# An eight-expert layer between attention and a token mixer: experts with few slots take their hidden parts two at a time

## The chip, the cores and the metric

The kernel runs on one core of a Trainium2 chip. Its time is device time in microseconds (us): the median of three runs before the change is 499.38 us (497.16 to 500.8). One profiled execution, 495.95 us long, gives all the rows below; its span from the first to the last instruction is 494.1 us.

## The reference, cut to what matters

Three layers follow each other: local attention, a mixture of experts, and a mixer over tokens and channels. The change is in the second, whose core is this:

```
for b in range(B):                     # B, S, D, E, F = 2, 768, 512, 8, 1024
    for s in range(S):
        e = fresh_e or prev_e          # arg max of the gate, or the expert of the token before
        p = softmax(logits[b, s])
        h = np.maximum(x[b, s] @ w1[e], 0.0)
        out[b, s] = p[e] * (h @ w2[e])
```

Each of the 1536 tokens goes to one of eight experts. An expert has a 512 by 1024 matrix `w1`, a relu, and a 1024 by 512 matrix `w2`.

## The kernel before, in words

**Slots.** The experts are ranked by how many tokens they have. Expert of rank `r` gets `RCAP[r]` slots: 288, 256, 256, 256, 192, 192, 160, 160. A tile of rows is 128 slots; rank 0 has three tiles, the others two. In ranks 4 to 7 the second tile has only 64 or 32 slots, and in rank 0 the third has 32. Ranks 4 to 7, with `N <= FEW = 192` slots, are the "few-slot" experts.

**Parts.** The 1024 hidden columns of an expert are eight parts of 128, so that the loop at L1564 runs over 64 units `u = 8 * r + f`. Weights come in pieces of two parts, 512 KB of `w1` and 512 KB of `w2` each, three buffers deep (`NRAW`). `load_piece` issues their DMAs on SP's queue: the `w1` half of a piece when the first products that read its last predecessor are issued, the `w2` half at the end of `mm2` of an odd unit.

**A unit, in program order.** Every engine executes its own instructions in this order; an order of different engines is set by semaphores alone.

- `mm1(u + 2)` (L1429): first products, slots as columns. In ranks 0 to 3 each is twelve TensorE products of split weights (L1454). In ranks 4 to 7 the raw float32 weights are used, four products that the trace shows as eight matmuls (L1438). Each unit takes a PSUM bank of its own from pool `pB`, which has two.
- `mm2(u)` (L1478): second products. A whole tile of rows takes three matmuls 512 columns wide (L1491) over the 128x128 array. A tile of 64 or 32 slots takes another form (L1501): the array is used as two or four column tiles side by side, each with 64 or 32 columns of weights, and each makes a part of the output columns (256 or 128). These are float32, and the trace shows two matmuls for each.
- `split_w1(u + 3)` and `split_w2(u + 1)`: ACT rounds the raw weights to a high half (L1324, L1421), DVE subtracts for the low half (L1325, L1422). Few-slot experts need no `split_w1`.
- `relu(u + 2)` (L1457): ACT makes the high half `hh` of the whole tiles (L1468), DVE the part tile `hx` (L1472) and the low half `hl` (L1473).
- `y_out(u)`: ACT scales a finished tile of the expert before, and issues its store.
- `tick()`, six times in a unit: 2.4 steps a unit (ranks 4 to 7) of a side job that decodes matrices of the third layer. A job is six steps, mostly DVE instructions on 128x512 (L396 to L408), an ACT copy at each end (L395, L405), and a DMA of the next 512 KB, issued on ACT's queue (L381).
- `x_tr(r + 1, i)` (L1287), at parts 2 and 3: four TensorE transposes of a tile of the next expert's rows (L1299), an ACT copy (L1302), and the gather of the tile three further on by GpSimd.

Ahead of the loop stand `mm1(0)`, `relu(0)`, `mm1(1)`, `split_w1(2)`, `split_w2(0)`, `relu(1)`, in this order (L1556 to L1561). `LOADS` (L74) orders the first weight DMAs after that of piece 0's `w1`: `(1, 1)` is the `w1` half of piece 1, `(0, 2)` the `w2` half of piece 0.

Of the kernel before, what the change touches and what calls it, by code (L numbers as in the profile page):

```python
# [38 lines left out]
FEW = 192  # L39
RBASE = [1, 4, 6, 8, 10, 12, 14, 16]  # L40
# [33 lines left out]
LOADS = ((1, 1), (0, 2), (1, 2), (2, 1), (2, 2))  # L74
# [14 lines left out]
def f32(ap):  # L89
    return ap.bitcast(F32)  # L90
# [3 lines left out]
def kernel(  # L94
# [887 lines left out]
    def load_piece(n, parts=(1, 2)):  # L982
# [4 lines left out]
        k = r if n else -1  # L987
        if k not in regs:
            regs[k] = SP.value_load(order_g[0:1, r : r + 1] if n else first_i, min_val=0, max_val=E - 1)
# [287 lines left out]
    wsp1, mb_, pR_ = {}, [], []  # L1277
# [9 lines left out]
    def x_tr(r, i, low=True):  # L1287
# [8 lines left out]
        tp = (pR_[0] if r else pZ).tile([128, 4, 128], F32, tag="tr", name="tr")  # L1296
# [45 lines left out]
    with ExitStack() as mctx:  # L1342
# [5 lines left out]
        pR_.append(pR)  # L1348
        pslot = {}
# [75 lines left out]
        hts = {}  # L1425

        hps = {}

        def mm1(u):  # L1429
# [4 lines left out]
            hp = pB.tile([128, 512], F32, tag="b", name="h")  # L1434
            if N <= FEW:
                x, o = f32(xTs[r][0]), u % 2
# [10 lines left out]
            else:  # L1447
                h1, l1 = wsp1.pop(u)
# [6 lines left out]
            hps[u] = hp  # L1455

        def relu(u):  # L1457
# [4 lines left out]
            hp = hps.pop(u)  # L1462
            hh = mb.tile([128, max(RCAP)], F32R, tag="hh", name="hh", bufs=4)
            hl = mb.tile([128, max(RCAP)], F32R, tag="hl", name="hl", bufs=4)
            n, hx = N // 128 * 128, None
            if width(r, RTILES[r] - 1) == 128:
                n = N
            A.activation(hh[:, :n], hp[:, :n], AF.Relu)  # L1468
            if n < N:

                hx = mb.tile([128, 64], F32, tag="hx", name="hx", bufs=4)
                V.tensor_scalar(hx[:, : N - n], hp[:, n:N], 0.0, None, op0=ALU.max)  # L1472
            V.scalar_tensor_tensor(hl[:, :n], hp[:, :n], 0.0, f32(hh[:, :n]), op0=ALU.max, op1=ALU.subtract)  # L1473
            hts[u] = (hh, hl, hx)

        yps = {}

        def mm2(u):  # L1478
# [4 lines left out]
            hh, hl, hx = hts.pop(u)  # L1483
            for i in range(RTILES[r]):
# [3 lines left out]
                c = width(r, i)  # L1488
                if c == 128:
# [8 lines left out]
                else:  # L1498
                    W = 4 * c
                    for g in range(128 // c):  # L1500
                        PE.matmul(  # L1501
                            out[g * c : g * c + M, :W],
                            lhsT=hx[:, :M],
                            rhs=w[:, g * W : (g + 1) * W],
                            start=(f == 0),
                            stop=(f == 7),
                        )
            if u % 2:
                pieces.pop(u // 2)
                load_piece(u // 2 + NRAW, (2,))  # L1510
# [480 lines left out]
```

## Time and profile before

| what | value |
|---|---|
| median of three runs | 499.38 us |
| profiled execution | 495.95 us, span 494.1 us |
| TensorE (PE) busy | 478.5 us, 97% of the span |
| VectorE (DVE) busy | 353.8 us, 72% |
| ScalarE (ACT) busy | 260.8 us, 53% |
| granted TensorE clock | 0.999 of full speed |
| DMA | 83.18 MB, 168 GB/s mean |

Busy shares are averages over three layers with different limits. The expert loop runs from about 121 to 309 us. Where rows give starts of consecutive TensorE instructions, the distance between starts is what an instruction takes of the engine; the duration printed beside it also holds the time in which the array empties and overlaps the next one.

### The profile page before, as it was taken

The page shows a single profiled execution, that of the slowest core. Times are in us where ns is not written, and L with a number is a line of the kernel's source. Part 1 is how long each engine was busy: PE and PEld are TensorE (multiplying, and loading weights), DVE is VectorE, ACT ScalarE, POOL GpSimd, SP SyncE. Part 2 cuts the span into 40 slices and gives each one's busy share as a digit, 9 for nine tenths or more (in the row PEclk, how much of TensorE's full clock was granted, in tenths as well). Part 3 has the DMA queues.
Part 4 walks back from the last instruction along what each step waited for, and adds up shares of the span by engine and source line. Part 5 has one row for each costly group of instructions (what it writes and reads, how often), then busy time and mean ns, then how long its engine had stood idle before and what let it go on. Part 6 is the DMA issues. An engine that isn't in the chain of part 4 may idle for free.

```text
span 494.1 us, 9501 instructions
## 1 busy us (share of the span) xinstructions
PE 478.5 (97%) x3328; PEld 385.0 (78%) x3330; DVE 353.8 (72%) x955; ACT 260.8 (53%) x634; POOL 117.4 (24%) x145
## 2 busy tenths in 40 slices
PE   8998998899999999999999999999999999999994
PEld 4676776678788899987777776888888888888884
DVE  6878878857665878777777888657999795751421
ACT  5977786732455756665455664555655354520300
POOL 4003214234105303021311102303453232430400
PEclk9999999999999999999999999999999999999999
DMA  8967578713949876976888995420012000000122
GB/s 244 350 191 247 178 242 248 227 44 114 337 63 299 287 255 227 303 253 225 297 278 288 305 312 174 142 98 22 23 64 72 15 23 21 2 34 32 34 96 69
DMA packets 62343, 83.18 MB, mean 168 GB/s; under 512 B 6496, under 2 KB 40928, under 8 KB 62288
## 3 DMA queue, kind: packets, MB, share of 16 engines
q1 hardware_dynamic: 53812, 61.97, 39.4%
q10 hardware_dynamic: 5708, 13.50, 8.0%
q0 software_dynamic: 2768, 7.02, 4.6%
q8 instruction: 28, 0.46, 0.4%
q14 instruction: 27, 0.22, 0.1%
HBM read 71.14 MB, written 11.34 MB: 167 GB/s over the span
## 4 chain that ended last, share of the span: by engine, by line
PE 79%; DVE 7%; DMA 6%; ACT 4%; issue 2%; ACTq 0%; SPq 0%; DVEq 0%; POOLq 0%
PE a L1746 21%; PE o L1491 11%; PE h L1454 8%; PE b L1783 7%; PE th L1670 6%; PE h L1438 6%; PE s L547 3%; PE x L626 3%; PE o L1501 3%; PE pt L602 2%; DVE sm L569 2%; DMA yd<-yo 2%; DMA jraw<-in_w_tokT_dram 2%; PE h L757 2%; PE y L768 2%
## 5 line engine op out<-in xcount | busy, mean ns | idle before, releaser
L1746 PE MATMUL a<-wtokr,z 128*128 128x512 f32 x480 | 87.1, 340 | 0.0
L1746 PEld LDWEIGHTS a<-wtokr,z 128*128 128x128 f32 x480 | 73.5, 188 | 10.7
L1491 PE MATMUL o<-w2s,hh 128*128 128x512 f32 x192 | 64.9, 417 | 0.7 <-DVE w2s L1422 0.4
L579 ACT ACTIVATE pr<-sm,st 128x256 f32<-128x256 f32 (+1 forms) x96 | 46.1, 482 | 19.9 <-DVE st L569 19.9
L1422 DVE TENSOR_TENSOR w2s<-raw,w2s 128x512 fp32r<-128x512 f32 x64 | 44.0, 688 | 14.7 <-ACT w2s L1421 14.6
L1454 PE MATMUL h<-xT,w1s 128*128 128x256 f32 (+1 forms) x384 | 53.4, 288 | 1.2 <-DVE w1s L1325 0.6
L1454 PEld LDWEIGHTS h<-xT,w1s 128*128 128x128 f32 x384 | 49.5, 188 | 4.3 <-DVE w1s L1325 1.1
L1438 PE MATMUL h<-xT,raw 128*128 128x192 f32 (+1 forms) x256 | 46.0, 323 | 0.0
L1438 PEld LDWEIGHTS h<-xT,raw 128*128 128x128 f32 x256 | 38.5, 190 | 7.0 <-issue 6.6
L1421 ACT ACTIVATE w2s<-raw 128x512 fp32r<-128x512 f32 x64 | 39.9, 623 | 7.6 <-ACT yo L1537 3.5
L569 DVE CUSTOM_DVE_ANT_0 sm<-s,bias 128x256 f32<-128x256 f32 (+1 forms) x96 | 34.0, 395 | 10.3 <-PE s L547 10.1
L1468 ACT ACTIVATE hh<-h 128x256 fp32r<-128x256 f32 (+1 forms) x64 | 20.8, 324 | 33.8 <-PE h L1454 18.9
L1491 PE MATMUL o<-w2s,hl 128*128 128x512 f32 x96 | 38.0, 395 | 0.0
L1491 PEld LDWEIGHTS o<-w2s,hh 128*128 128x128 f32 x192 | 33.0, 189 | 5.2 <-DVE w2s L1422 1.2
L1012 POOL DMA_INDIRECT xg<-xd,xidx x17 | 16.8, 986 | 85.0 <-PE tr L1299 78.6
L602 PE MATMUL pt<-ident,pr 128*128 128x128 f32 x176 | 26.0, 280 | 4.5 <-DVE xt L652 3.2
L1325 DVE TENSOR_TENSOR w1s<-raw,w1s 128x512 fp32r<-128x512 f32 x32 | 22.1, 690 | 9.6 <-ACT w1s L1324 9.4
L1791 DVE SCALAR_TENSOR_TENSOR ob<-b,xTf 128x512 f32<-128x512 f32 (+1 forms) x16 | 8.8, 556 | 27.6 <-PE b L1783 27.5
L1702 POOL TENSOR_TENSOR si<-si,yg 128x512 f32<-128x512 f32 x10 | 13.4, 1343 | 60.0 <-ACT si L1695 50.8
L1473 DVE SCALAR_TENSOR_TENSOR hl<-h,hh 128x256 fp32r<-128x256 f32 (+1 forms) x64 | 22.4, 350 | 6.0 <-ACT hh L1468 6.0
L602 PEld LDWEIGHTS pt<-ident,pr 128*128 128x128 f32 x176 | 19.2, 141 | 9.4 <-DVE xt L652 3.8
L547 PE MATMUL s<-kall,q 64*128 64x256 f32 (+1 forms) x192 | 25.6, 385 | 0.0
(266 smaller groups left out, 951.3 us busy)
## 6 DMA issues: line engine op xcount, KB each, us to landing
raw<-in_w_dram SPq DMA_DIRECT2D x64, 512.0 KB, 5.2
vv<-in_pack_dram SPq DMA_DIRECT2D x10, 512.0 KB, 5.7
jraw<-in_w_tokT_dram ACTq DMA_DIRECT2D x10, 512.0 KB, 4.7
w<-in_w_dram SPq DMA_DIRECT2D x16, 256.0 KB, 6.6
kall<-in_pack_dram SPq DMA_DIRECT2D x10, 320.0 KB, 4.4
xd<-xt SPq DMA_DIRECT2D x12, 256.0 KB, 2.1
q<-in_pack_dram SPq DMA_DIRECT2D x11, 256.0 KB, 4.5
yd<-yo ACTq DMA_DIRECT2D x11, 256.0 KB, 4.1
```

What stands on the lines that cost most here:

```text
L547: PE.matmul(sp[hh][:, 0:W], lhsT=qs[n][half, j], rhs=kall[half, b, j, t * 160 + 160 - W : t * 160 + 160], start=True, stop=True,)
L569: V.tensor_tensor_reduce(out=sm[:, hh, 0:W], in0=ust[u]["s"][hh], in1=bias[:, 2 * j + hh], scale=-0.125, scalar=BIG, op0=ALU.add, op1=ALU.min,
L579: A.activation(pr[:, hh, 0:W], sm[:, hh, 0:W], AF.Exp, bias=st[:, hh : hh + 1], scale=-1.0, accum_out=sums[n][:, 2 * j + hh : 2 * j + hh + 1],
L602: PE.transpose(pt[:, hh, c], pr[:, hh, c * 128 : (c + 1) * 128], ident)
L1421: A.activation(h2, bb[:, o], AF.Copy)
L1422: V.tensor_tensor(l2, bb[:, o], f32(h2), op=ALU.subtract)
L1438: PE.matmul(hp[:, :N], lhsT=pieces[u // 2][1][:, j, o * 128 : (o + 1) * 128], rhs=x[:, j, :N], start=(j == 0), stop=(j == 3),)
L1454: PE.matmul(hp[:, :N], lhsT=wa[:, j], rhs=xa[:, j, :N], start=(k == 0), stop=(k == 11))
L1491: PE.matmul(out[:M], lhsT=ha[:, lo : lo + M], rhs=wa, start=(f == 0 and q == 0), stop=(f == 7 and q == 2),)
L1670: PE.matmul(th, lhsT=xa[:, j], rhs=wa[:, j], start=(n == 0), stop=(n == 11))
L1746: PE.matmul(acc[b][d][o], lhsT=za[:, d * 128 : (d + 1) * 128], rhs=wa[:, lo:hi], start=(t == 0 and n == 0 and (o == 0 or d % 2 == 0)), sto ...
L1783: PE.matmul(op[:, : hi - lo], lhsT=wa[:, d, e * 128 : (e + 1) * 128], rhs=ua[d][:, lo:hi], start=(n == 0), stop=(n == 11),)
```

## The change

Part tiles are multiplied for two parts in a row, everywhere: `mm2` does the whole tiles alone, and a new `mm2_few` does the part tile of units `u` and `u + 1`. In ranks 0 to 3 it is called at the end of `mm2` of an odd unit. In ranks 4 to 7 the loop body runs for a pair of units at once: both `mm1`, both `mm2`, then `mm2_few`. A pair's first products share a bank (two halves of 256 columns), and one ACT and two DVE instructions do the relu of both. `split_w2` runs two units ahead. Both tiles of the next expert's rows are transposed at part 2, the second one into a bank of pool `pO`. The twelve ticks of a pair remain twelve.

Beside this, `LOADS` puts the `w2` half of piece 0 ahead of the `w1` half of piece 1, and at `u = 0` the call `mm1(2)` stands behind `mm2(0)`. The lines ahead of the loop are the same.

```diff
+FEW0 = 4
-LOADS = ((1, 1), (0, 2), (1, 2), (2, 1), (2, 2))
+LOADS = ((0, 2), (1, 1), (1, 2), (2, 1), (2, 2))
...
-        k = r if n else -1
+        k = r if n or parts != (1,) else -1
...
-        tp = (pR_[0] if r else pZ).tile([128, 4, 128], F32, tag="tr", name="tr")
+        if r > FEW0 and i:
+            tp = pO_[0].tile([128, 4, 128], F32, tag="o", name="tr")
+        else:
+            tp = (pR_[0] if r else pZ).tile([128, 4, 128], F32, tag="tr", name="tr")
...
         def mm1(u):
-            hp = pB.tile([128, 512], F32, tag="b", name="h")
+            o = u % 2
             if N <= FEW:
-                x, o = f32(xTs[r][0]), u % 2
+                if o == 0:
+                    hps[u] = pB.tile([128, 2, 256], F32, tag="b", name="h")
+                hp = hps[u - o][:, o]
+                x = f32(xTs[r][0])
...
         def relu(u):
+            few = N <= FEW
+            if few and u % 2 == 0:
+                return
+            hp = hps.pop(u - 1 if few else u)
...
+            if few:
+                dh, dl = [x[:, : 2 * n].rearrange("p (i c) -> p i c", i=2) for x in (hh, hl)]
+                A.activation(dh, hp[:, :, :n], AF.Relu)
+                V.tensor_scalar(hx[:, :, : N - n], hp[:, :, n:N], 0.0, None, op0=ALU.max)
+                V.scalar_tensor_tensor(dl, hp[:, :, :n], 0.0, f32(dh), op0=ALU.max, op1=ALU.subtract)
+                for o in range(2):
+                    hts[u - 1 + o] = hh[:, o * n : o * n + n], hl[:, o * n : o * n + n], hx[:, o]
+                return
...
+        def mm2_few(u):
+            r = u // 8
+            i = RTILES[r] - 1
+            c, M, out = width(r, i), RCAP[r] - i * 128, yps[r][i]
+            for v in (u, u + 1):
+                hx, w = fews.pop(v)
+                for g in range(128 // c if c < 128 else 0):
+                    PE.matmul(
+                        out[g * c : g * c + M, : 4 * c],
+                        lhsT=hx[:, :M],
+                        rhs=w[:, 4 * g * c : 4 * (g + 1) * c],
+                        start=(v % 8 == 0),
+                        stop=(v % 8 == 7),
+                    )
+            pieces.pop(u // 2)
+            load_piece(u // 2 + NRAW, (2,))
...
+            if RCAP[r] > FEW:
+                if u:
+                    mm1(u + 2)
+                mm2(u)
+                if u % 2:
+                    mm2_few(u - 1)
+                if u == 0:
+                    mm1(2)
...
+            elif u % 2 == 0:
+                mm1(u + 2)
+                mm1(u + 3)
+                if f == 2 and r < 7:
+                    for i in range(2):
+                        x_tr(r + 1, i)
+                mm2(u)
+                mm2(u + 1)
+                mm2_few(u)
+                split_w2(u + 2)
+                for _ in range(3):
+                    tick()
+                relu(u + 3)
+                for _ in range(3):
+                    tick()
+                split_w2(u + 3)
+                y_out(u)
+                for _ in range(6):
+                    tick()
+                y_out(u + 1)
```

## Rows read from the trace of the kernel before

**Rows 1.** Page, busy time of each engine: us, share of span, instructions.

```profile
PE 478.5 (97%) x3328; PEld 385.0 (78%) x3330; DVE 353.8 (72%) x955; ACT 260.8 (53%) x634; POOL 117.4 (24%) x145
```

**Rows 2.** Stretches of the expert loop: length, busy per engine, clock, DMA share, GB/s.

```profile
121.00:170.00 49.00, 47.25 (x340) 38.80 (x338) 31.03 (x71) 26.09 (x55) 12.80 (x12) 1.00 0.80 240
...
222.00:267.00 45.00, 45.00 (x253) 33.46 (x251) 33.86 (x82) 23.35 (x51) 8.72 (x8) 1.00 0.82 272
267.00:304.00 37.00, 37.00 (x293) 27.25 (x290) 31.35 (x82) 23.29 (x51) 4.51 (x5) 1.00 0.88 293
```

**Rows 3.** Waits of TensorE, 121 to 310 us: line, releaser, total, times, longest.

```profile
PE h L1454 <- DVE w1s L1325: 0.6, 2, 0.4
...
PE o L1491 <- DVE w2s L1422: 0.4, 2, 0.2
```

**Rows 4.** Timeline of TensorE, around rank 4's first units: start, duration, what.

```profile
221.53 1.46 PE L1438 MATMUL h<-xT,raw 128*128 128x192 f32 x8
222.69 0.75 PE L1491 MATMUL o<-w2s,hh 128*128 128x512 f32 x2
223.28 0.39 PE L1491 MATMUL o<-w2s,hl 128*128 128x512 f32 x1
223.51 0.62 PE L1491 MATMUL o<-w2s,hh 128*128 128x512 f32 x2
...
228.65 0.40 PE L1491 MATMUL o<-w2s,hl 128*128 128x512 f32 x1
228.98 0.65 PE L1501 MATMUL o<-raw,hx 128*64 128x256 f32 x4
229.56 1.57 PE L1438 MATMUL h<-xT,raw 128*128 128x192 f32 x8
230.83 0.76 PE L1491 MATMUL o<-w2s,hh 128*128 128x512 f32 x2
```

**Rows 5.** The same timeline in rank 6.

```profile
274.30 0.43 PE L1501 MATMUL o<-raw,hx 128*32 128x128 f32 x8
274.65 1.35 PE L1438 MATMUL h<-xT,raw 128*128 128x160 f32 x8
...
276.64 0.42 PE L1501 MATMUL o<-raw,hx 128*32 128x128 f32 x8
```

**Rows 6.** Chain of waits at 118 us: float32 products 128 (L757), 256 (L768) wide.

```profile
118.39 0.89 PE h L757 x8
119.28 1.73 PE y L768 x8
```

**Rows 7.** The same chain at the loop's start: start, us, what.

```profile
122.01 5.90 DMA raw<-in_w_dram
...
128.65 0.70 DVE w2s L1422
...
129.40 1.43 PE o L1491 x5
```

**Rows 8.** Timelines of ACT and TensorE there; brackets: idle before, releaser.

```profile
125.00 0.62 ACT L1324 ACTIVATE w1s<-raw 128x512 fp32r<-128x512 f32 x1
127.99 0.63 ACT L1421 ACTIVATE w2s<-raw 128x512 fp32r<-128x512 f32 x1 [2.36 <-DMA raw<-in_w_dram]
...
125.03 3.33 PE L1454 MATMUL h<-xT,w1s 128*128 128x288 f32 x23 [0.21 <-DVE w1s L1325]
128.67 0.50 PE L1491 MATMUL o<-w2s,hh 128*128 128x512 f32 x1 [0.31 <-ACT w2s L1421]
...
131.12 1.86 PE L1454 MATMUL h<-xT,w1s 128*128 128x288 f32 x12
```

**Rows 9.** Chain of waits and TensorE's timeline, late in the loop.

```profile
280.55 7.76 DMA jraw<-in_w_tokT_dram
...
288.34 0.68 ACT jm L395
...
306.68 0.50 PE L1491 MATMUL o<-w2s,hh 128*128 128x512 f32 x1 [0.18 <-DVE w2s L1422]
```

More of the change, by code (lines that the diff above doesn't have):

```diff
@@ L1348 @@
         pR_.append(pR)
+        pO_.append(pO)
         pslot = {}
@@ L1447, in mm1 @@
             else:
+                hps[u] = hp = pB.tile([128, 512], F32, tag="b", name="h")
                 h1, l1 = wsp1.pop(u)
@@ L1461, in relu @@
             N = RCAP[r]
[L1462 removed]
+            n = N // 128 * 128
+            if width(r, RTILES[r] - 1) == 128:
+                n = N
+            few = N <= FEW
+            if few and u % 2 == 0:
+                return
+            hp = hps.pop(u - 1 if few else u)
             hh = mb.tile([128, max(RCAP)], F32R, tag="hh", name="hh", bufs=4)
             hl = mb.tile([128, max(RCAP)], F32R, tag="hl", name="hl", bufs=4)
[L1465 to L1467 removed]
+            if n < N:
+                if few or u % 2 == 0:
+                    hxs[0] = mb.tile([128, 2, 64], F32, tag="hx", name="hx", bufs=2)
+                hx = hxs[0]
+            if few:
[6 more added lines that the diff above has]
+                return
             A.activation(hh[:, :n], hp[:, :n], AF.Relu)
             if n < N:
[L1471 to L1472 removed]
+                V.tensor_scalar(hx[:, u % 2, : N - n], hp[:, n:N], 0.0, None, op0=ALU.max)
             V.scalar_tensor_tensor(hl[:, :n], hp[:, :n], 0.0, f32(hh[:, :n]), op0=ALU.max, op1=ALU.subtract)
[L1474 to L1476 removed]
+            hts[u] = hh, hl, hx[:, u % 2] if n < N else None
+        yps, fews = {}, {}
         def mm2(u):
@@ L1497, in mm2 @@
                         )
[L1498 to L1510, printed above, removed]
+        def mm2_few(u):
[14 more added lines that the diff above has]
+            load_piece(u // 2 + NRAW, (2,))
         def y_out(u):
@@ L1571, in tick @@
                     quick[0] %= 1
-            mm1(u + 2)
-            mm2(u)
-            tick()
-            split_w1(u + 3)
-            tick()
-            split_w2(u + 1)
-            tick()
-            tick()
-            relu(u + 2)
-            tick()
-            tick()
-            y_out(u)
+            if RCAP[r] > FEW:
[7 more added lines that the diff above has]
+                tick()
+                split_w1(u + 3)
+                tick()
+                split_w2(u + 1)
+                if u == 8 * FEW0 - 1:
+                    split_w2(u + 2)
+                tick()
+                tick()
+                relu(u + 2)
+                tick()
+                tick()
+                y_out(u)
[8 more added lines that the diff above has]
+                mm2_few(u)
+                split_w2(u + 2)
+                for _ in range(3):
+                    tick()
+                relu(u + 3)
+                for _ in range(3):
+                    tick()
+                split_w2(u + 3)
+                y_out(u)
+                for _ in range(6):
+                    tick()
+                y_out(u + 1)
             if GX <= u < GX + RTILES[0]:
@@ L1609 @@
             i = f - (2 if r else XF)
-            if r < 7 and 0 <= i < RTILES[r + 1]:
+            if r < FEW0 and 0 <= i < RTILES[r + 1]:
                 x_tr(r + 1, i)
```

12 lines of the change are left out of this document (5 added, 7 removed).

## The prediction

> **What bounds the kernel now.** I read the engines' busy times first: TensorE is at 97%, DVE at 72%, ACT at 53% [rows 1]. A share over three layers says little, so the expert loop was cut into stretches next. From 222 to 304 us, where the few-slot experts run, TensorE is busy all the time at full clock; DVE is busy for 31.35 of the last 37.00 us and the DMA engines are at 0.82 and then 0.88 [rows 2]. TensorE's waits in the whole loop are some 0.4 to 0.6 us each and most stand at its start [rows 3]. So in this loop a change is worth what it takes off TensorE, as long as the next two (DVE, then DMA, in the last two ranks) keep up. The change leaves the number of matmuls as it is. What remains is their order, so I then read TensorE's timeline for what an order costs: the distances between starts.
>
> **What a change of form costs.** The products over the whole array follow each other at 0.23 us (223.28 to 223.51). From the last of them to the first of the part tile there are 0.33 us (228.65 to 228.98): **0.10 us going in**. Eight first products take 1.16 us behind a whole-array product (221.53 to 222.69) and 1.27 us behind a part tile (229.56 to 230.83): **0.11 us coming out** [rows 4]. Inside, the part tile of rank 4 takes 0.58 us (228.98 to 229.56) [rows 4], that of rank 6 0.35 us (274.30 to 274.65) [rows 5]. Elsewhere float32 products of 256 columns run at 1.73 / 8 = 0.216 us and those of 128 at 0.89 / 8 = 0.111 us [rows 6]. With two column tiles at once rank 4's four matmuls would stream in 2 x 0.216 = 0.43 us, with four at once rank 6's eight in 2 x 0.111 = 0.22 us; the rest, 0.15 and 0.13 us, is filling and emptying at the ends, if it isn't inherent in the form.
>
> Two part tiles in a row drop one going in and one coming out, 0.21 us for certain by these rows, and of the rest between nothing and 0.15 us. A merge is thus worth 0.21 to 0.36 us. I take 0.30, nearer to the upper end, because the rows with full streaming are of the same engine and type.
>
> **The sum, part by part.**
>
> - *Merges in ranks 4 to 7*: 32 units, 16 merges, all on the path: 16 x 0.30 = **-4.8 us** (bounds -3.4 and, with 0.36 and 0.34 for the two forms, -5.6).
> - *Merges in rank 0*, which has a part tile of 32 slots: 4 x 0.30 = **-1.2 us** (-0.8, -1.4). The other three ranks have none.
> - *Paired relu*: 32 instructions each of three kinds become 16 of double width. ACT and DVE save part of this, but TensorE waits for neither there [rows 3]: nothing by itself. The even part's relu now waits for the odd part's first products, some 1.2 us [rows 4]; its cover is what lies up to its use, the second products and the part tiles of the pair and the first products of the next, about 4.3 us of the 2 x 2.34 us that a pair takes (274.30 to 276.64) [rows 5]. Queued behind the waiting relu on ACT and DVE are six ticks, a `w2` split and the stores; TensorE needs that split some 4 us later.
> - *Transposes*: the same eight a time, moved ahead of the pair's second products. They no longer stand behind a part tile; both orders change form as often within 0.1 us, three times: nothing. ACT's queue stops for them until the pair's first products are done, where the relu would have stopped it. The second bank comes from `pO`, whose last user there was scaled out two pairs earlier. GpSimd's gathers follow them, three tiles ahead of need: nothing.
> - *Weight DMAs*: each half is issued once in a pair as before, the `w2` half after the merged part tiles. SP is moved past nothing else. The `w2` split needs it two pairs later. Nothing, while DMA keeps up.
> - *DVE and DMA in the last two ranks*: a pair that goes from 4.68 to 4.38 us meets 31.35 / 37.00 x 4.68 = 4.0 us of DVE work, and a DMA share of 0.88 that becomes 0.94 [rows 2, 5]. One side-job load there took 7.76 us to land, and ACT took it up at once when it had (288.34) [rows 9]: what shortens a pair here is partly waited for again. I give back 40% of these eight merges: **+1.0 us** (0 to +2.4). The 0.18 us that TensorE waits for a split `w2` at 306.68 [rows 9] should go, since the splits run earlier: **-0.2 us**.
> - *The loop's start.* Before, the `w1` half of piece 1 is split on ACT at 125.00; then ACT idles 2.36 us until the `w2` half of piece 0 has landed, 5.90 us after its issue [rows 7, 8]. TensorE meanwhile does `mm1(1)` and `mm1(2)`, 23 of whose matmuls follow 125.03 without a break in 3.33 us (12 of them some 1.6 us, without the last one's emptying), and waits 0.31 and 0.23 us beside that. With the DMAs exchanged (SP still loads the same two registers, the second of them before the first of these DMAs, as now), `w2` lands first, but `split_w1(2)` still stands ahead of `split_w2(0)` in ACT's order, and its half now lands second. If that is at 127.99 again, ACT does 0.62 + 0.63 us, DVE two subtractions of 0.70 us [rows 7, 8], so that the second of the products now at 129.40 comes at about 130.05: 0.65 us later; and the 1.6 us of `mm1(2)`, which filled the wait, come behind it: +2.25 us in all. If the second half lands by about 126 us, where the first products of part 1 end, only some 0.15 us are lost. Between these, since a load of 512 KB at the 240 GB/s of this stretch [rows 2] needs 2.2 us behind one that landed by 125.0: landing at 127.2, **+1.4 us** (0.15 to 2.25).
>
> In all -4.8 - 1.2 + 1.0 - 0.2 + 1.4 = **-3.8 us**, from 495.95 us of the profiled execution to 492.1 us. That execution is 3.4 us under the median shown, 499.38 us; on the median's scale the forecast is **495.6 us**.
>
> **A rule against it.** The Trainium skill, "PSUM — Partial Sum Buffer", section "PSUM bank collisions raise a hardware error", says that two engines must not touch one bank in the same 32 partitions at once, even at other columns, so sharing a bank forces the relu of the first half to wait for the second. No run here shows a bank touched by two; the rows show only that the wait of 1.2 us has about 4.3 us of cover. By the rule alone, with that wait on the path in each of 16 pairs, the sum would come out 16 x 1.2 = 19 us the other way; by the rows it comes to nothing.
>
> **The rivals.**
>
> *The start is not late and every merge counts.* The half lands early (+0.15) and all 20 merges give their full value, 8 x 0.36 + 12 x 0.34 = 7.0 us: -7.0 + 0.15 - 0.2 = -7.0 us, 492.4 us. For it: two loads issued within a microsecond may land nearly together. Against: 125.0 and 127.9 before [rows 7, 8].
>
> *The extra belongs to the narrow form, and the start is late.* Merging then gives 0.21 a time, the last two ranks give back half of theirs, and the start costs 2.25: -4.2 + 0.8 + 2.25 = -1.1 us, 498.2 us: the change would not do what it says, as far as can be measured. For it: no row shows two part tiles in a row. Against: the 0.11 us depend on what stood before, for the same matmuls [rows 4].
>
> *The relu comes too late (slower).* In the last two ranks, a pair's relu is released at once for both parts, behind a `w2` split and ticks on ACT and DVE; DVE's work of 4.0 us a pair and the cover of 4.3 us lie close. When ACT waits for a side-job load as late as 7.76 us [rows 9], the relu passes its cover. It decides from a delay of 4.3 us on. If TensorE waits 0.5 us in each of 16 pairs: -6.0 + 8.0 + 1.4 = +3.4 us, 502.8 us. For it: ACT met that load just in time. Against: before, the cover was of the same size, and TensorE waited 0.18 us in it.
>
> **How the numbers follow.** Forecast 0.50, first rival 0.22, second 0.20, third 0.08. One per cent, 5 us, is about what a measurement of this kernel can tell from no change. Under 494.4 us lie a quarter of the forecast's case (its own range is 493.2 to 497.8) and most of the first rival's: 0.33. Over 504.4 us lies part of the third: 0.06. The rest is 0.61. The range that holds 8 in 10 goes from 491.8 us, 0.6 us under the first rival, to 499.6 us, which takes in the second rival.
>
> **What would show it.** In the trace after: distances between starts of 8 part-tile matmuls of rank 4 in a row (1.0 us forecast, 1.16 if nothing but the ends is saved); first products behind them at 1.27 once a pair and 1.16 the other time; a pair in some 5.2 us in rank 4 and 4.4 in rank 6; `mm2(0)`'s second product at about 130 us or later, and `mm1(2)` behind it; waits of TensorE for `hl` or `w2s` in ranks 6 and 7 if the third rival holds; the landing time of side-job loads there. Wrong would be the forecast if the part tiles in a row kept 0.58 and 0.35 us each with all their ends, if TensorE waited over 1 us in the last ranks, or if the start lost nothing.

## The result, and the profile after

The changed kernel takes **501.45 us** (median of 12 runs, 496.89 to 504.25) beside 499.01 us (496.66 to 501.0) of the kernel before on the same chip: **1.0064 times as long, with a 95% interval of 1.0041 to 1.0086**. That is within the 1% that the prediction called no change, but the interval leaves out 1, the sign is the other one, and the time lies above the range (491.8 to 499.6 us). The profiled execution of after has 501.50 us and a span of 499.7 us, 5.6 us more than before (494.1 us).

The two profiled executions are not alike: that of after lies at its median, that of before (495.95 us) under the lowest of its twelve runs. By the medians the change costs 2.4 us, by the ratio 3.2 us; the rows below explain the 5.6 us between these two executions. The granted clock of TensorE is part of what differs from run to run. Its median is 0.9885 in the twelve runs of after, and 0.994 to 0.997, by chip, in the runs of the kernel before that stand beside the experiments. A clock lower by 0.0075 (0.996 less 0.9885) for 500 us can cost 3.75 us at most (an estimate), as much as the whole difference.

On the page, the busy times and the row of the granted clock by slices of 12.5 us (in tenths; 9 stands for 0.9 and more):

```profile
PE 479.0 (96%) x3328; PEld 390.6 (78%) x3330; DVE 349.2 (70%) x923; ACT 259.0 (52%) x618; POOL 115.9 (23%) x145
...
PEclk9999999999799999999999999999999999999999
```

Against [rows 1], ACT and DVE have lost the 16 and 32 instructions of the paired relus, and TensorE is as busy as before. New is the 7 in the clock's row: the slice that begins at 125 us. Three stretches of the loop, to be laid beside [rows 2] (length, busy time and count of PE, PEld, DVE, ACT, POOL, clock, DMA share, GB/s):

```profile
121.00:137.00 16.00, 12.40 (x64) 10.43 (x63) 6.75 (x16) 5.59 (x13) 2.88 (x3) 0.79 0.83 283
222.00:267.00 45.00, 45.00 (x264) 37.18 (x263) 31.44 (x65) 22.85 (x45) 8.71 (x9) 1.00 0.85 281
267.00:304.00 37.00, 36.53 (x293) 28.91 (x293) 31.39 (x69) 21.39 (x43) 2.68 (x3) 1.00 0.90 298
```

From 222 to 267 us more matmuls fit into the same time (264 for 253): the merges work. At the start the clock is down to 0.79, and late in the loop TensorE idles. Its waits from 115 to 320 us say for whom (line, releaser, total, times, longest), beside [rows 3]:

```profile
PE o L1513 <- ACT w2s L1427: 3.0, 1, 3.0
PE tr L1403 <- DVE hit L1398: 0.9, 1, 0.9
PE o L1513 <- DVE w2s L1428: 0.7, 2, 0.5
PE o L1513 <- DVE hl L1488: 0.6, 1, 0.6
...
```

One wait of 3.0 us is new at the start; the three rows below it all stand in rank 7. Where the 5.6 us arise is read from the starts of a few TensorE instructions, `mm1(u)` standing for the first product of unit `u`. Here and below such starts are rounded to 0.1 us before they are subtracted, so that a difference is good to 0.1 us:

| span, us | before | after | difference |
|---|---|---|---|
| up to `mm1(4)` | 134.6 | 139.5 | +4.9 |
| `mm1(4)` to `mm1(32)`, ranks 0 to 3 | 86.9 | 85.9 | -1.0 |
| `mm1(32)` to `mm1(56)`, ranks 4 to 6 | 65.6 | 62.5 | -3.1 |
| `mm1(56)` to the third layer's first product | 21.8 | 25.3 | +3.5 |
| from there to the end | 185.2 | 186.5 | +1.3 |

**The start.** ACT's timeline and TensorE's (start, duration, what; in brackets the idle time before and its releaser), to be laid beside [rows 8]:

```profile
128.70 0.63 ACT L1329 ACTIVATE w1s<-raw 128x512 fp32r<-128x512 f32 x1 [3.33 <-DMA raw<-in_w_dram]
129.24 0.61 ACT L1427 ACTIVATE w2s<-raw 128x512 fp32r<-128x512 f32 x1
```

```profile
123.10 3.85 PE L1463 MATMUL h<-xT,w1s 128*128 128x288 f32 x24 [0.49 <-ACT xT L1309]
129.90 1.61 PE L1513 MATMUL o<-w2s,hh 128*128 128x512 f32 x2 [2.95 <-ACT w2s L1427]
131.31 0.63 PE L1513 MATMUL o<-w2s,hl 128*128 128x512 f32 x1
131.73 1.05 PE L1513 MATMUL o<-w2s,hh 128*128 128x512 f32 x2
132.59 0.63 PE L1513 MATMUL o<-w2s,hl 128*128 128x512 f32 x1
133.01 4.61 PE L1463 MATMUL h<-xT,w1s 128*128 128x288 f32 x24
```

ACT waits until 128.70 us for the half of piece 1, because its split stands first in ACT's order; the split of `w2`, whose data came first, follows at 129.24. TensorE, left without `mm1(2)`, idles for 2.95 us, and the granted clock falls to half (1.2 GHz instead of 2.4 GHz) for 6.8 us from 129.0 us: two matmuls of 512 columns, then 0.62 us, take 1.05, and 24 first products take 4.45 us (to 137.46).

**The merged part tiles** of rank 4 and rank 6, beside [rows 4, 5]:

```profile
234.87 1.08 PE L1529 MATMUL o<-raw,hx 128*64 128x256 f32 x8
235.88 0.43 PE L1446 MATMUL h<-xT,raw 128*128 128x192 f32 x1
...
296.95 0.64 PE L1529 MATMUL o<-raw,hx 128*32 128x128 f32 x16
297.53 2.44 PE L1446 MATMUL h<-xT,raw 128*128 128x160 f32 x16
```

Eight in a row take 1.01 us (234.87 to 235.88) where twice four took 1.16; sixteen take 0.58 us (296.95 to 297.53) where twice eight took 0.70.

### The profile page after: what moved, and what is told of

The parts are those of the page before. It is cut to its first block, busy times and chain, and to the rows that moved or that the text cites. A ratio compares the mean times of both kernels' runs of the same rounds, so it can differ in the third digit from the quotient of the medians.

```text
span 499.7 us, 9450 instructions
## 1 busy us (share of the span) xinstructions
PE 479.0 (96%) x3328; PEld 390.6 (78%) x3330; DVE 349.2 (70%) x923; ACT 259.0 (52%) x618; POOL 115.9 (23%) x145
## 4 chain that ended last, share of the span: by engine, by line
PE 69%; DVE 10%; DMA 8%; ACT 7%; issue 3%; SPq 1%; ACTq 1%; DVEq 0%; POOLq 0%
PE a L1803 17%; PE o L1513 10%; PE h L1463 8%; PE b L1840 7%; PE th L1727 5%; PE h L1446 4%; PE x L627 3%; PE s L548 3%; PE pt L603 2%; DMA yd<-yo 2%; DMA jraw<-in_w_tokT_dram 2%; PE h L758 2%; PE y L769 2%; PE o L1529 2%; ACT pr L580 1%
## 5 line engine op out<-in xcount | busy, mean ns | idle before, releaser
L1463 PEld LDWEIGHTS h<-xT,w1s 128*128 128x128 f32 x384 | 51.0, 193 | 3.9 <-DVE w1s L1330 1.0
L1513 PEld LDWEIGHTS o<-w2s,hh 128*128 128x128 f32 x192 | 34.1, 192 | 11.3 <-ACT w2s L1427 3.6
L1446 PE MATMUL h<-xT,raw 128*128 128x192 f32 (+1 forms) x256 | 42.4, 318 | 0.0
L1513 PE MATMUL o<-w2s,hl 128*128 128x512 f32 x96 | 39.0, 406 | 0.6 <-DVE hl L1488 0.6
L1492 ACT ACTIVATE hh<-h 128x256 fp32r<-128x256 f32 x32 | 12.2, 381 | 23.9 <-PE h L1463 23.8
L627 PE MATMUL x<-ps,vv 128*64 128x128 f32 x352 | 24.5, 279 | 0.0
```

The lines of the kernel that those rows point to most:

```text
L627: PE.matmul(xp[64 * hh : 64 * hh + 64, j], lhsT=vv[:, i, h * 64 : (h + 1) * 64], rhs=ps[:, hh, c], start=(c == 0), stop=(c == nch - 1),)
L1446: PE.matmul(hp[:, :N], lhsT=pieces[u // 2][1][:, j, o * 128 : (o + 1) * 128], rhs=x[:, j, :N], start=(j == 0), stop=(j == 3),)
L1463: PE.matmul(hp[:, :N], lhsT=wa[:, j], rhs=xa[:, j, :N], start=(k == 0), stop=(k == 11))
L1513: PE.matmul(out[:M], lhsT=ha[:, lo : lo + M], rhs=wa, start=(f == 0 and q == 0), stop=(f == 7 and q == 2),)
```

## The experiments

All eighteen runs in one table; starts are those of the profiled execution. "Ratio" is the time over that of the kernel before on the same chip, with its 95% interval. "Rank 7" is the time from `mm1(56)` to the third layer's first product. In the names, "pair" is the order of the change and "merge" that of single units. The quoted texts, written before each run, name their theories by letters; E changes its meaning: up to merge_w2_first_pool_copy it says that the job's loads land late, from pair_w2_pool on that DVE's own work is too much.

| kernel | time, us | ratio | `mm1(4)` | `mm1(56)` | rank 7 | span |
|---|---|---|---|---|---|---|
| pair_only | 498.17 | 1.0015 (0.9988 to 1.0042) | 137.0 | 285.6 | 25.1 | 497.2 |
| start_only | 503.25 | 1.0127 (1.0084 to 1.0171) | 137.4 | 289.7 | 22.6 | 497.9 |
| start_w2_first | 497.92 | 1.0005 (0.9982 to 1.0028) | 134.9 | 284.1 | 24.5 | 495.1 |
| start_filled | 499.41 | 1.0033 (0.9998 to 1.0068) | 135.8 | 287.7 | 25.5 | 499.8 |
| merge_only | 494.73 | 0.9937 (0.991 to 0.9964) | 135.9 | 284.3 | 23.8 | 493.0 |
| w2_first_fewer_steps | 497.92 | 0.9985 (0.9956 to 1.0014) | 136.7 | 286.3 | 20.4 | 495.9 |
| before_fewer_steps | 504.03 | 1.0119 (1.0081 to 1.0157) | 136.2 | 289.5 | 21.3 | 501.0 |
| pair_early_steps | 501.13 | 1.0066 (1.0035 to 1.0096) | 135.2 | 290.0 | 23.2 | 498.9 |
| merge_early_steps | 496.25 | 0.995 (0.992 to 0.9979) | 134.3 | 290.0 | 20.5 | 495.6 |
| merge_w2_first_early_steps | 495.3 | 0.9948 (0.9922 to 0.9974) | 134.2 | 285.7 | 21.4 | 491.9 |
| pair_pool_copy | 494.82 | 0.9951 (0.9926 to 0.9975) | 133.4 | 281.8 | 24.7 | 493.0 |
| pair_steps_last | 498.16 | 1.002 (1.0003 to 1.0036) | 134.3 | 282.7 | 24.5 | 495.7 |
| merge_w2_first | 493.53 | 0.9923 (0.9885 to 0.9961) | 133.9 | 282.6 | 23.9 | 491.7 |
| merge_w2_first_pool_copy | 494.64 | 0.9961 (0.9937 to 0.9985) | 135.0 | 283.3 | 24.1 | 492.7 |
| pair_w2_pool | 501.12 | 1.005 (1.0015 to 1.0085) | 135.7 | 285.3 | 27.1 | 499.2 |
| merge_w2_pool | 497.7 | 0.9976 (0.9945 to 1.0007) | 133.9 | 284.6 | 26.9 | 497.3 |
| merge_w2_pool_all | 499.52 | 1.0011 (0.9979 to 1.0044) | 136.1 | 287.9 | 26.7 | 499.8 |
| pair_less_dve | 495.35 | 0.99 (0.9835 to 0.9965) | 136.1 | 285.0 | 22.4 | 494.9 |

### Which half costs the time: the start or the pairs

pair_only is the changed kernel with the start as before; start_only is the kernel before with the exchanged start.

```diff
 # pair_only
-LOADS = ((0, 2), (1, 1), (1, 2), (2, 1), (2, 2))
+LOADS = ((1, 1), (0, 2), (1, 2), (2, 1), (2, 2))
...
-                if u:
-                    mm1(u + 2)
+                mm1(u + 2)
...
-                if u == 0:
-                    mm1(2)
```

> The change with its start undone: the old order of the first weight DMAs, and mm1(2) ahead of mm2(0) again. Theory A (the exchanged start makes TensorE idle 2.95 us, the granted clock falls to half for 6.8 us behind it, and nothing later gives that back): mm1(4) starts near 135 us as in the kernel before, no half clock near 129 us, and the time falls 4 to 5.5 us under the changed kernel's, to within 2.5 us of the kernel before. Theory B (the end of the loop is set by the chain of side jobs, DVE and DMA, whatever the start): mm1(4) is early, but the loop ends at 312 to 313 us all the same, and the time stays within 1.5 us of the changed kernel's.

> The kernel before with the exchanged start alone (order of the first weight DMAs, mm1(2) behind mm2(0)). Theory A: TensorE idles about 3 us after mm1(1), the clock is halved for some 7 us from about 129 us, mm1(4) starts near 139.5 us and the time is 4 to 5.5 us over the kernel before. Theory B: the loop's later stages absorb it; at most 1.5 us over the kernel before.

Taking the start back brings the ratio from 1.0064 to 1.0015: the start costs some 0.5%, about 2.5 us (4 to 5.5 were expected). In the kernel before the same start costs 1.27%, 6.3 us, by five runs. But the pairs without it are no gain, which was not expected: 25.1 us in rank 7, as in the change.

The old start is not always as good as in the profile of before, either. In pair_only ACT had the `w2` half of piece 0 only at 129.11 us (127.99 before), TensorE idled for 1.93 us, and 3.4 us at half clock followed from 131.6 us, so that `mm1(4)` came at 137.0 us and not at the 135 expected. So the 4.9 us at the start are measured against an execution in which this half landed early. In start_only the gap was 2.21 us and its profiled execution shows no half clock there; it is the fastest of its five runs.

### The start: the order of two splits, and the clock

start_w2_first is the changed kernel with two calls exchanged; start_filled leaves their order and puts 22 matmuls, whose result nobody reads, into TensorE's gap.

```diff
 # start_w2_first
         mm1(1)
+        split_w2(0)
         split_w1(2)
-        split_w2(0)
         relu(1)
```

```diff
 # start_filled
         relu(1)
+        fill_ps = pR.tile([128, 4, 128], F32, tag="tr", name="fill")
+        for _ in range(22):
+            PE.matmul(fill_ps[:, 0:2], lhsT=w1h[:, 0], rhs=xTs[0][0][:, 0, 0:256], start=True, stop=True)
```

> The changed kernel with one swap ahead of the loop: split_w2(0) stands before split_w1(2). Theory A, in its version that the order on ACT and DVE holds the landed w2 half back behind the one that lands later: mm2(0) starts near 127 us instead of 129.9, mm1(2) near 130 us, TensorE's gap is under 1.5 us, the clock stays full, mm1(4) at 135 to 136 us; time 3.5 to 5 us under the changed kernel's. If instead the landing of the DMAs decides whatever the order, mm2(0) stays near 130 us and the time within 1 us of the changed kernel's.

> The changed kernel with 22 matmuls of 256 columns between mm1(1) and mm2(0), whose results nobody reads, so that TensorE is busy in most of its gap; all its waits stay. If the half clock is what the idle gap brings (theory A), the clock stays full from 121 to 170 us, mm2(0) still starts at about 130 us, mm1(4) at 136 to 136.5 us instead of 139.5, and the time is some 3 us under the changed kernel's. If the half clock has another cause, it stands at 129 us again and the time is the changed kernel's within 1 us.

TensorE's timeline of start_filled, where the first row is the filling:

```profile
126.47 2.79 PE L1592 MATMUL fill<-xT,w1s 128*128 128x256 f32 x22
129.10 0.72 PE L1513 MATMUL o<-w2s,hh 128*128 128x512 f32 x2
129.66 0.40 PE L1513 MATMUL o<-w2s,hl 128*128 128x512 f32 x1
129.89 0.62 PE L1513 MATMUL o<-w2s,hh 128*128 128x512 f32 x2
130.35 0.39 PE L1513 MATMUL o<-w2s,hl 128*128 128x512 f32 x1
130.57 3.35 PE L1463 MATMUL h<-xT,w1s 128*128 128x288 f32 x24
```

With the gap filled the order on ACT is as before, yet the matmuls keep their full speed (0.62 us, 3.18 us for 24) and `mm1(4)` starts at 135.8 instead of 139.5 us. Not all of this is the clock: the half of piece 1 also landed earlier here (ACT takes it up at 127.31 instead of 128.70 us), so that `mm2(0)` starts 0.8 us earlier, at 129.10. From `mm2(0)` to `mm1(4)` the same matmuls take 6.70 us here and 9.61 us in after: **the clock costs 2.9 us**. The other 2.0 of the 4.9 us are the order and the late landing. Splitting `w2` first removes both: `mm2(0)` at 126.23 us and `mm1(4)` at 134.9. Its time is 1.0005 of before, 2.9 us under that of the change by the ratios, where 3.5 to 5 were expected. start_filled as a whole gained about 1.5 us, half of what was expected, since half clock came elsewhere in its profile: 3.4 us from 171.8, behind another gap of 1.93 us, and 6.8 us from 308.4.

### The merges alone

merge_only is the kernel before, with the part tiles of two units in a row and nothing else: one unit at a time, a bank and a relu for each. `mm2_few` is that of the change; its text is left out here.

```diff
 # merge_only
...
             mm2(u)
+            if u % 2:
+                mm2_few(u - 1)
             tick()
```

> The kernel before, unit by unit, its start and relus untouched, with the part tiles of two units multiplied in a row at the end of each odd unit (20 merges). By the prediction's price a merge is worth 0.30 us (0.21 to 0.36), 6 us in all. Theory A (the merges pay, and it is the order of a pair on ACT and DVE that gives them back at the loop's end): rank 7 runs no later than the others, and the time falls 3 to 6 us under the kernel before. Theory B (a shorter expert loop is given back by DVE and DMA in the last rank whatever the order): by the start of rank 7 it is 3 us ahead, at the loop's end level, and the time is within 1 us of the kernel before.

**0.9937**: 3.1 us under the kernel before, and faster than both kernels. The three ranks 4 to 6 take 61.95 us instead of 65.56: 3.6 us for 12 merges, 0.30 each, the value that the prediction took. So the merges are right, and what eats their gain in rank 7 is already here, to a lesser degree: 23.8 us, where 21.8 - 5 x 0.30 = 20.3 are due.

### Rank 7: what makes TensorE wait

In rank 7 the side job's steps were the first suspect. Two kernels stop the job at unit 56 (the third layer then has to do those steps itself), three do more of it in ranks 4 and 5 and less in rank 7.

```diff
 # w2_first_fewer_steps (from start_w2_first), before_fewer_steps
-JL = 61
+JL = 56
 # pair_early_steps (from start_w2_first), merge_early_steps, merge_w2_first_early_steps
-JRATE = (0, 1.3, 1.3, 1.3, 2.4, 2.4, 2.4, 2.4)
+JRATE = (0, 1.3, 1.3, 1.3, 2.8, 2.8, 2.4, 1.4)
```

> The changed kernel with split_w2(0) ahead of split_w1(2) as in the run start_w2_first, and without side-job steps in rank 7 (they move to the third layer). Theory C (the last rank ends late because some 19 steps on DVE and ACT, 2.4 a unit, stand between the relus and splits that TensorE waits for): TensorE's waits in rank 7 fall from some 2.5 us to under 0.5, no half clock near 309 us, rank 7 from its first mm1(56) to the loop's end takes 20 to 21 us instead of 24.5, and the time is 2 to 4 us under start_w2_first, if the third layer hides the steps; if it does not, the layer grows by 1 to 2 us. Rival (the order of the pair itself, its relu released late): rank 7 keeps its waits of 2 us and more, and the time stays within 1 us of start_w2_first.

> The kernel before, without side-job steps in rank 7: the control for the run w2_first_fewer_steps. TensorE waits 0.18 us there as it is, so rank 7 should shorten by 0.5 us at most, and the time show only what the steps cost in the third layer: between 0 and 2 us more than the kernel before under theory C as under its rival.

> The changed kernel with split_w2(0) ahead of split_w1(2), and with the side job's rate moved forward: 2.8 steps a unit in ranks 4 and 5, 2.4 in rank 6, 1.4 in rank 7, about as many in all as before (71 against 70). Theory C (the steps on DVE and ACT in rank 7 hold up the pair's relus and splits): rank 7 from mm1(56) to the loop's end takes 21 to 22.5 us instead of 24.5, ranks 4 and 5 stay at 21.8 us, the third layer does not grow, and the time is 2 to 4 us under the kernel before. Rival (the pair's order itself is late in rank 7): 24 us and more in rank 7, and the time within 1 us of the kernel before.

> The run merge_only with the same shift of the side job's rate. Theory C: rank 7, which took 23.8 us with merges alone against 21.8 in the kernel before, takes 20.5 to 21.5; time 5 to 6.5 us under the kernel before. Rival: rank 7 stays above 23 us, time as merge_only's, some 3 us under the kernel before.

> merge_early_steps with the exchanged start and split_w2(0) ahead of split_w1(2). From mm1(0) to mm1(4) the old start took 11.8 to 14.7 us in the profiles so far, this one 10.8 to 12.2: if it spares the idle gap in those runs in which the w2 half lands late, the time is 0.5 to 1.5 us under merge_early_steps; if the half's landing does not matter once the merges are in, they are equal within 0.5 us.

Without the steps rank 7 takes 20.4 us in w2_first_fewer_steps, about the 20.3 that are due: it is the steps. But the time is not had that way (0.9985 and 1.0119; 2 to 4 us under start_w2_first and at most 2 us over before were expected). The third layer's main products, 145.3 us before (317.0 to 462.3), take 148.8 us in w2_first_fewer_steps and 150.2 us in before_fewer_steps, there with 3.4 us at half clock. Earlier steps were a miss in all three kernels: rank 7 falls to 20.5 us in merge_early_steps, but `mm1(56)` starts at 290.0 instead of 284.3 us, so ranks 5 and 6 are late instead. The job's work was paid for wherever it was put.

The change also gives rank 7 more of these steps, which the prediction did not see. Its twelve ticks of a pair do remain twelve, but a tick counts only while `u < JL = 61`: with single units the job stops after unit 60, while the pair that begins at unit 60 runs all its twelve. DVE does 19 instructions of the job in rank 7 in after and in start_w2_first, 15 in before and in merge_only (62 instead of 60 in ranks 4 to 7 as a whole). At some 0.6 us each, the two added ones alone are 1.2 us of DVE (an estimate). No run takes just these away.

The steps load both ACT and DVE. First I held that the two block each other (theory D in the texts quoted): ACT's waits for the job's last bit step, in front of its copy, from 222 to 313 us, are 9.4 us before, 18.4 us after and 18.7 us in start_w2_first. Two edits test it, one that does the copy on GpSimd and one that puts all ticks of a pair behind its splits and its relu.

```diff
 # pair_pool_copy (from start_w2_first), merge_w2_first_pool_copy (from merge_w2_first);
 # shortened: the new order holds in the expert loop only
-        A.activation(wh, wf, AF.Copy)
-        job_load()
+        G.tensor_copy(wh, wf)
         yield
+        job_load()
 # pair_steps_last (from start_w2_first): split_w2, relu, split_w2, y_out, then
-                for _ in range(6):
+                for _ in range(12):
                     tick()
```

> start_w2_first with the side job's copy of the high half moved from ACT to GpSimd while the expert loop runs, and the next load issued a step later. In the pair order ACT waits for the side job's DVE steps for 18.7 us between 222 and 313 us (9.4 in the kernel before), and the w2 splits queue behind it. Theory D (ACT and DVE hold each other up through the job's copy): ACT's waits for DVE's job steps fall under 5 us, rank 7 takes 21.5 to 23 us instead of 24.5, time 1.5 to 3 us under start_w2_first. Theory E (the job's late loads hold both up): rank 7 stays within 0.7 us of 24.5, time within 1 us of start_w2_first.

> start_w2_first with a pair's twelve ticks behind both w2 splits and the relu, instead of three ahead of the relu, three behind it and six behind the first store. No step is taken out or moved to another engine. Theory D, in which what TensorE needs stands behind job steps: TensorE's waits in rank 7 (some 2.5 us) fall below 1 us and rank 7 takes 22 to 23 us. Theory E: no change in rank 7 beyond 0.7 us, since the loads are as late as before.

> merge_w2_first with the job's copy on GpSimd. In merge_only ACT waited 13.9 us for the job's DVE steps and rank 7 took 23.8 us against 21.8 before. Theory D: rank 7 in 21 to 22 us, time 1.5 to 2.5 us under merge_w2_first. Theory E: within 1 us of it.

By its time pair_pool_copy seems to bear this out. Its trace does not: ACT waits for that step only 6.9 us (in rank 7 5.4 us, 8.3 in start_w2_first), but rank 7 takes 24.7 us, at most 0.8 of it by 1.5 us at half clock, and TensorE waits 3.0 us there (2.75 in start_w2_first). What is earlier is earlier ahead of rank 7 (133.4 us at `mm1(4)`, 24.8 instead of 25.7 us in rank 1, which takes 25.0 in after too). Why the kernel is faster over all its runs stays open; their median granted clock was 0.997, that of start_w2_first 0.993. In single units the copy on GpSimd brings nothing (0.9961, the interval crosses that of merge_w2_first).

pair_steps_last gained nothing either. There TensorE's waits for `w2s` and `hl` in rank 7 are gone, but one of 2.33 us for `hit`, which stands behind job steps on DVE, has come in their place, with 3.4 us at half clock from 303.1 us. DVE's timeline of pair_pool_copy in rank 7 shows what is left, with one row of TensorE's:

```profile
298.14 0.22 DVE L1493 TENSOR_SCALAR hx<-h 128x64 f32<-128x64 f32 x1
298.28 0.41 DVE L1494 SCALAR_TENSOR_TENSOR hl<-h,hh 128x256 fp32r<-128x256 f32 x1
298.61 0.84 DVE L1434 TENSOR_TENSOR w2s<-raw,w2s 128x512 fp32r<-128x512 f32 x1
299.37 0.68 DVE L415 TENSOR_TENSOR wtokr<-jw,wtokr 128x512 fp32r<-128x512 f32 x1
300.08 0.45 DVE L397 TENSOR_SCALAR jw<-jraw 128x512 int32<-128x512 int32 x1
300.56 0.69 DVE L399 SCALAR_TENSOR_TENSOR jw<-jraw,jw 128x512 int32<-128x512 int32 x1
301.17 0.15 DVE L1403 CAST slot<-yidx 128x1 f32<-128x1 int32 x1
301.43 0.29 DVE L1404 TENSOR_SCALAR hit<-hit,slot 128x128 f32<-128x128 f32 x1
301.63 0.69 DVE L1434 TENSOR_TENSOR w2s<-raw,w2s 128x512 fp32r<-128x512 f32 x1
...
301.77 0.33 PE L1409 MATMUL tr<-ident,hit 128*128 128x128 f32 x1 [0.88 <-DVE hit L1404]
```

No row of DVE has a bracket: it goes from one instruction to the next, here and from 289.1 to 304.5 us, and TensorE waits for its results (`hit`, then `hl` and `w2s`). So the second theory (E): **DVE's own work is what a shorter rank 7 has no room for.** Three kernels give the subtraction for odd units' second weights to GpSimd, from unit 55 on or (the last) from 33 on:

```diff
 # pair_w2_pool (from start_w2_first), merge_w2_pool and, with 32, merge_w2_pool_all (from merge_w2_first)
-            V.tensor_tensor(l2, bb[:, o], f32(h2), op=ALU.subtract)
+            (G if o and u >= 54 else V).tensor_tensor(l2, bb[:, o], f32(h2), op=ALU.subtract)
```

> The order of start_w2_first; the subtraction for the low half of the odd units' second weights is done by GpSimd from unit 55 on, five times, instead of DVE. Nothing else changes; the job and its copy on ACT stay. Theory E (DVE's own work sets the end of rank 7; 5 x 0.60 us leave its queue): rank 7, from the first products of unit 56 to the third layer's first product, falls from 24.5 us to some 22 us, TensorE's waits for DVE's instructions there fall from 2.75 us to under 1 us, and the time is some 2 us under that of start_w2_first: 0.996 of the kernel before. Theory D (ACT and DVE hold each other up by the job's copy): nothing of that changes, rank 7 stays at 24 to 25 us and the time at 1.000.

> The same in the order of single units: merge_w2_first, with the same five subtractions on GpSimd. Theory E: rank 7 falls from 23.9 us to some 21.5 us, and the time from 0.9923 to some 0.988 of the kernel before. Theory D: no change, 0.992.

> merge_w2_first with the subtractions of all odd units from 33 on, sixteen, on GpSimd. Theory E: as merge_w2_pool, since TensorE waits for nothing in ranks 4 to 6: 0.988. Against it: GpSimd issues the gathers of rows and scales there, and one behind a subtraction comes later by 1.3 us; three tiles ahead of need that costs nothing. Theory D: 0.992.

All three are misses: 2.6 to 3.0 us longer in rank 7 (in two of them up to 1.5 and 1.7 us of that by half clock). TensorE's waits in rank 7 and the timelines of GpSimd and of DVE in pair_w2_pool say why:

```profile
PE o L1513 <- POOL w2s L1428: 2.0, 3, 0.9
PE o L1513 <- DVE hl L1488: 1.9, 1, 1.9
PE tr L1403 <- DVE hit L1398: 0.4, 1, 0.4
```

```profile
303.15 1.27 POOL L1428 TENSOR_TENSOR w2s<-raw,w2s 128x512 fp32r<-128x512 f32 x1 [3.01 <-ACT w2s L1427]
...
306.99 1.27 POOL L1428 TENSOR_TENSOR w2s<-raw,w2s 128x512 fp32r<-128x512 f32 x1
```

```profile
303.31 1.40 DVE L397 TENSOR_SCALAR jw<-jraw 128x512 int32<-128x512 int32 x1
...
306.65 2.18 DVE L401 SCALAR_TENSOR_TENSOR jw<-jraw,jw 128x512 int32<-128x512 int32 x1
308.75 0.21 DVE L1487 TENSOR_SCALAR hx<-h 128x64 f32<-128x64 f32 x1
```

While GpSimd subtracts, a job step of DVE takes 1.40 instead of 0.43 us and 2.18 instead of 0.69. Five of them lose 5.0 us in all (0.61, 0.96, 0.97, 0.97, 1.49), and five subtractions of 0.60 us save 3.0: DVE has 2.0 us more to do, and `hl` is late behind the step of 2.18 us. Beside that TensorE now waits 2.0 us for GpSimd itself. The load was not taken off, and a wait of another kind was added, so this does not test the theory. The last run takes work off DVE and puts it nowhere. It leaves out two of a job's four bit steps in units 54 to 61; what is decoded there is wrong.

```diff
 # pair_less_dve (from start_w2_first)
-        V.scalar_tensor_tensor(w, lo, 29, w, op0=ALU.logical_shift_right, op1=ALU.bitwise_or)
+        if not 54 <= jstate.get("u", 0) < 62:
+            V.scalar_tensor_tensor(w, lo, 29, w, op0=ALU.logical_shift_right, op1=ALU.bitwise_or)
```

(The step two lines below, that of sign and exponent, is treated in the same way.)

> The order of start_w2_first; in units 54 to 61 two of a job's four bit steps on DVE are left out (the merge of the low word and that of the sign and exponent), so that the third-layer weights decoded there are wrong and only the time counts. About six instructions of 0.60 us leave DVE's queue, 3.6 us; ACT's copies, the loads and the number of steps stay. Theory E (DVE's own work sets rank 7): rank 7 falls from 24.5 us to 21 to 22 us, TensorE's waits there from 2.75 us to under 1 us, and the time to some 0.995 of the kernel before. Theory D (the order in which ACT and DVE wait for each other by the copy): the copy still stands behind the job's last bit step; rank 7 falls by less than 1 us and the time stays at 1.000.

Rank 7 takes **22.4 us instead of 24.5**, and the ratio is 0.99 (0.9835 to 0.9965). TensorE's waits from 281 to 312 us, first in start_w2_first, then in pair_less_dve:

```profile
PE o L1513 <- DVE w2s L1428: 1.2, 3, 0.5
PE tr L1403 <- DVE hit L1398: 0.9, 1, 0.9
PE o L1513 <- DVE hl L1488: 0.6, 1, 0.6
```

```profile
PE o L1515 <- DVE w2s L1430: 0.7, 2, 0.5
PE o L1515 <- ACT hh L1488: 0.2, 1, 0.2
PE tr L1405 <- DVE hit L1400: 0.2, 1, 0.2
```

2.7 us of waits become 1.1, while most of ACT's own waits for the job stay (15.3 us instead of 18.7; in rank 7 6.1 instead of 8.3). pair_pool_copy shortened those waits more and left rank 7 as it was. Both speak for DVE's work as the cause and for ACT's waits as a companion, and theory D had forecast less than 1 us. The two are not fully parted: in neither run are ACT's waits in rank 7 gone, and a DVE step left out also shortens what ACT waits for.

The waits of rank 7 can cost twice. A half clock of 3.4 or 6.8 us begins between 303 and 310 us in after, pair_only, start_filled, pair_pool_copy, pair_steps_last, pair_w2_pool and merge_w2_pool, where TensorE waits 2.0 to 4.4 us in rank 7; none does in before, merge_only and merge_w2_first, where it waits 0.2 to 1.6 us. It does not follow each time: start_w2_first waits 2.75 us and merge_w2_pool_all 4.5 us without it.

### The version that beats both

merge_w2_first joins what paid: the kernel before, the merges, the exchanged start, and `split_w2(0)` ahead of `split_w1(2)`. Its edits are those of merge_only, start_only and start_w2_first.

> The kernel before with merges and with the exchanged start whose w2 split stands first, the side job as it was. Merges alone gave -3.1 us; if the start of this form spares an idle gap now and then, -3.5 to -5 us against the kernel before; if it is worth nothing, -3 us within 1 us.

493.53 us, **0.9923 (0.9885 to 0.9961)**, with a span of 491.7 us. The units stay single, so that a relu is released half a pair earlier. Its interval overlaps that of merge_only (0.991 to 0.9964): that the start adds to the merges is not shown by the times. In the profiles `mm1(4)` comes at 133.9 instead of 135.9 us.

## Why the prediction was wrong

- **Merges in ranks 4 to 7 and 0: right.** 0.30 a merge was forecast, 0.30 measured in merge_only for ranks 4 to 6, and 1.01 us for eight in a row (1.0 forecast). In the pairs the three ranks gave 3.1 us of the 3.6 due; where the 0.5 us went was not followed.
- **The loop's start: the step that failed first.** The forecast was +1.4 us (0.15 to 2.25). The order of landing and splitting came as described, and it is worth 2.0 us, inside these bounds. What the term left out is the granted clock: with TensorE's gap of 2.95 us came 6.8 us at half clock, 2.9 us more. All of it together was +4.9 us between the two profiles, over twice the upper bound. (Against runs in which the old start had its gap too, as in pair_only, the start costs some 2.5 us.) [Rows 2] showed the clock at 1.00 in these stretches, and I took it as given where I was adding a gap.
- **DVE in the last two ranks: mis-sized, the second step that failed.** The term gave back +1.0 us (0 to 2.4). In rank 7 alone TensorE lost 3.5 us where some 1.2 to 1.5 us were to be gained, some 5 us beside the forecast; 1.6 us of the loss lie at half clock from 309.9 us on. In the times it is the larger of the two: pair_only, without the new start, is at 1.0015, where the forecast without its start term was -5.2 us, about 0.99. The 4.0 us of DVE work for a pair of 4.38 us was a mean over two ranks, and the room between them is not usable: DVE waits in order for ACT's splits (for one of them 1.62 us, behind the job's copy, in start_w2_first), and rank 7 has `hit` of its own and, in the pairs, more steps of the job on top (19 instructions of DVE instead of 15). The prediction's own sign, TensorE waiting over 1 us in the last ranks, came true with 2.2 us. The wait of 0.18 us at 306.68 [rows 9], which was to go, became 0.7 us of waits for `w2s`.
- **Paired relu, transposes, weight DMAs at nothing:** right up to rank 7. `hl` is waited for once, 0.6 us in the last pair; the transposes nowhere. Rank 7 is 24.5 us in pairs and 23.9 in single units, with the same start; whether the relu, released half a pair later, or the added job steps make this difference, no run shows.
- **The rivals.** The third had the right place (DVE's load and cover lie close in the last ranks) and nearly the right time, 502.8 us, which was luck, since the mechanism was wrong: not each of 16 pairs waits for its relu, and no side-job load is at fault; ACT waits for one for 1.3 us once. The rule against it, that two parts in one bank make a relu wait, can be read from the same rows: this wait stayed under its cover in all pairs but the last.

The sum by its measured terms: +4.9 - 1.0 - 3.1 + 3.5 + 1.3 = +5.6 us, where -3.8 was forecast. The last term, behind the loop, was in no step. Some 0.6 us of it are a longer wait of TensorE for a gathered row (`yg`, 0.76 instead of 0.20 us, just ahead of the main products) and some 0.6 us a longer run of these products (145.9 instead of 145.3 us); what makes the row and the products later stays open. The half clock of 309.9 us ends at 313.3 us and has next to no part in it.

## What to carry to other kernels

Before an edit opens a gap in a busy TensorE, price the clock as well as the gap, and look at the order in which the engine that feeds it takes up what has landed. DVE was busy for 85% of the last stretch, in its own order and with others waiting for it; that was as good as full, since a stage that was to become some 6% shorter was paid for by waits. When steps are grouped in pairs, look at where a loop's limit cuts them: here the last pair ran two units' ticks where one had run. When a change has several parts, run each of them alone; here the one part that pays (-0.6%) was hidden by two that did not. And when the time of one kernel differs by 1% from run to run, compare the profiled execution with the median before its rows are added up.

## What the runs showed of the hardware that was not expected

- Gaps of TensorE of 1.93 us (pair_only) and 2.95 us (after) came with 3.4 and 6.8 us at half clock; one of 1.75 us (merge_only) and one of 2.21 us (start_only) with none in the profiled run. But that run of start_only, at a mean granted clock of 0.996, is its fastest; the other four had 0.987 to 0.994 and were 1.9 to 4.7 us slower. So the price of a gap varies from execution to execution.
- Each of five GpSimd subtractions of two 128x512 operands stretched one of the DVE instructions beside it by 0.6 to 1.5 us, the float copy of pair_pool_copy hardly (a subtraction at 298.61 took 0.84 instead of 0.69 us). The Trainium skill, "SBUF — State Buffer", section "SBUF: two separate sides", says that the pair of ports that the two engines share goes to one instruction at a time; the rows agree for the steps with two inputs, and show the same for L397, which reads one tensor (1.40 us at 303.31). Where a job step kept its time beside a subtraction (L399 at 291.93, L397 at 297.19 us), the subtraction is the longer one: 1.83 and 1.57 instead of 1.27 us.
- Leaving this work to GpSimd was therefore no relief for DVE here (5.0 us lost for 3.0 saved), though GpSimd is idle three quarters of the time.
